# Scatters behind the casts, a third row buffer, the weights' parts moved, and drains between pages

## Chip, core and metric

The kernel runs on one core of one Trainium2 chip. The metric is the device time of one execution in microseconds (us), lower being better. TensorE is PE in the rows, VectorE DVE, ScalarE ACT, GpSimd POOL, SyncE SP; each works through its own instructions in order. DMAs are issued by SP (queue q1), by ACT for two first loads, and by GpSimd (queue q0).

## What is computed

Blockwise causal attention (8 batches, 8 heads, 576 positions, head size 64), whose output is the input of a mixture of 8 experts: each of 4608 rows goes to the one expert with the largest gate logit.

```python
scores = np.where(mask, scale * np.matmul(q, k.transpose(0, 1, 3, 2)), -1e9)  # mask: blocks of 64
attn_out = softmax(scores) @ v
x = attn_out.transpose(0, 2, 1, 3).reshape(B * S, H * D)        # 4608 x 512
logits = x @ w_gate
expert_idx, gate_w = argmax(logits), softmax(logits) at expert_idx
h = np.maximum(x_sorted[lo:hi] @ w1[e], 0.0)                     # rows of expert e: 512 -> 1024
y_sorted[lo:hi] = h @ w2[e]                                      # 1024 -> 512
out = gate_w[:, None] * y                                        # in the rows' first order
```

## The kernel before

Two stages overlap at their ends. The **attention stage** goes through 32 pairs of heads, four to a batch (`HP` = 4). Iteration `p` of the main loop does, in this order: loads ahead (`load_v` for pair p+4, `load` of q and k for pair p+6, all on SP; v's last 64 positions come for a whole batch in `load_v4`), GpSimd's `cast` of pair p+2 into the one buffer `h16`, the scatters and the loads of weights, `scores` of pair p+1, `attend`, `keep` and `sums` of pair p, TensorE's transposes of `h16` (`trans`, pair p+2), then `turn_back` and `finish` of pair p-1, which write the pair's 128 columns into the row buffer `x16s` of its batch, and at last `logits`, `denominators` and `settle` (a transpose by VectorE of the strip `sB`, line 323).

A batch is routed while the next is computed: `weigh` in step 0, `choose` in step 1, `ranks`, `gates` and `slots` in step 2 (iteration 4b+7 for batch b). After `slots` the batch's 576 rows, of 258 words each, go to the region of their expert in `xsorted`, by five indirect DMAs of GpSimd (`scatter`, lines 404 to 413): parts 0 and 1 at the end of step 2, parts 2 to 4 in step 3, ahead of the weights but behind that iteration's cast, and the parts 0 and 1 stand ahead of it. There are two row buffers, so batch b+2 writes what batch b's scatters read.

The weights are cast to half precision by GpSimd's DMAs, in 32 parts of 512 KB as written (`load_weights`, four to an expert): 24 parts in the attention stage, the other 8 in the first pages. `wall` holds them all, and the places of the last two experts are lent to attention until their parts come. `xsorted`'s first rows are cleared by one DMA (`clear_heads`).

Near the end of attention the first 20 pages (`FIRST`) are planned from the counts of batches 0 to 5: `first_counts` (VectorE), `first_turns` (five operations of GpSimd), `first_behind` (a comparison of VectorE, then a product of GpSimd), `first_rows` (VectorE). The first eight page loads (`mload`: a transposing DMA and a small one) are issued by SP in iteration 31; the very first waits for all scatters issued by then (`behind_all`), and the others stand behind it in SP's queue.

The **page stage** runs 36 to 63 pages of 128 rows. `page(T)` does the first product of page T (`m1`, 32 matmuls), stages the weights of page T+2 (`mstage`), does the second product of page T-1 (`m2`, 8 matmuls), whose result ScalarE writes to one of five `y` and GpSimd scatters to the output, and loads page T+6. The rows of batches 6 and 7 are routed beside the first pages.

Of the kernel before, what the change touches and what calls it, by code (L numbers as in the profile page):

```python
# [8 lines left out]
F32 = mybir.dt.float32  # L9
# [8 lines left out]
ROW = 258  # L18
# [4 lines left out]
def kernel(  # L23
# [30 lines left out]
    def sb(name, shape, dtype=F32):  # L54
        return pool.tile(shape, dtype, name=name)
# [20 lines left out]
    h16 = sb("h16", [128, 9, 128], F16)  # L76
    qkTs = [sb(f"qkT{i}", [128, 2, 576], F16) for i in range(2)]
    pts = [sb(f"pt{i}", [128, 2, 1408]) for i in range(2)]
    accs = [sb("acc", [128, 2, 640]),
            wall[:, E - 1, 8:16, :].rearrange("p a f -> p (a f)").bitcast(F32)[  # L80
                :, 0:1280].rearrange("p (h q) -> p h q", h=2)]
    p4s = [sb(f"p4_{i}", [128, 2, 64]) for i in range(2)]
    vts = [sb(f"v{i}", [128, 4, 2, 64]) for i in range(3)] + [
        guest[:, 2304 + i * 512:2816 + i * 512].rearrange("p (c h d) -> p c h d", c=4, h=2)
        for i in range(2)]
# [1 line left out]
    v4s = [sb("v4", [128, H, 64]), guest[:, 3328:3840].rearrange("p (h d) -> p h d", h=H)]  # L87
    oTs = [sb(f"oT{i}", [128, 640]) for i in range(2)]
    lr = sb("lr", [128, 160])
    x16s = [sb(f"x16_{i}", [128, 5, ROW], I32) for i in range(2)]  # L90
    lgp = sb("lgp", [128, 5, H, E])
    ohs = [sb(f"oh{i}", [128, 5, E], F16) for i in range(2)]
    recs = [sb(f"rec{i}", [128, 5, 2]) for i in range(2)]
# [59 lines left out]
    def tmp(name, w=E, dtype=F32):  # L153
        if name not in small:
            small[name] = sb(name, [128, w] if isinstance(w, int) else list(w), dtype)
        return small[name]
# [35 lines left out]
    def load_v4(b):  # L192
        nc.sync.dma_start(out=v4s[b % 2][64:128],
                          in_=v[b, :, 512:576, :].rearrange("h p d -> p h d"))
# [144 lines left out]

    def finish(p):  # L340
        b, hp = p // HP, p % HP
        x16 = x16s[b % 2].bitcast(F16)
        nc.vector.tensor_tensor(  # L343
            out=x16[:, :, hp * 128:hp * 128 + 128].rearrange("p i (h d) -> p i h d", h=2),
            in0=back[:, 0:640].rearrange("p (i h d) -> p i h d", h=2, d=64),
            in1=recs[p % 2].unsqueeze(3).to_broadcast([128, 5, 2, 64]), op=ALU.mult)
# [29 lines left out]
        nc.scalar.activation(tmp("ex", (128, 5, E)), tmp("d", (128, 5, E)), AF.Exp)  # L376

    def gates(b):
        x16, ex, sm = x16s[b % 2], tmp("ex", (128, 5, E)), tmp("sm", 5)
        nc.vector.reduce_sum(out=sm, in_=ex, axis=AX.X)  # L380
        nc.vector.reciprocal(x16.bitcast(F32)[:, :, 256], sm)
        nc.vector.tensor_single_scalar(x16[:, :, 257], ids, float(b * S), op=ALU.add)
# [20 lines left out]

    def scatter(b, j):
        m = 128 if j < 4 else 64
        slot = tmp(f"slot{j}_{b % 2}", 1, I32)
        nc.gpsimd.tensor_single_scalar(slot, small[f"sl{b % 2}"][:, j:j + 1], 128.0, op=ALU.add)  # L407
        did = nc.gpsimd.indirect_dma_start(  # L408
            out=xsorted[:, :],
            out_offset=bass.IndirectOffsetOnAxis(ap=slot[0:m, :], axis=0),  # L410
            in_=x16s[b % 2][0:m, j, :], in_offset=None)
        apart("rows", did)
        tc.declare_no_dep(did.ins, group="closed pages", reason="rows of pages not yet closed")

# [227 lines left out]
    with tc.manual_schedule(engines={ET.PE, ET.Activation, ET.DVE, ET.Pool, ET.SP}):  # L642
# [3 lines left out]
        load_v(0)  # L646
        load(2)
        load_v(1)
        nc.scalar.activation(warm, ident32[0:64, 64:65], AF.Exp)
        for _ in range(28):  # L650
            nc.tensor.transpose(sA16[:, 0:128], ident16, ident16)
# [8 lines left out]
        for h in range(2):  # L660
# [1 line left out]
            nc.sync.dma_start(  # L662
                out=gate[r], in_=moe_w_gate.rearrange("(p h d) e -> h d p e", h=2, d=64)[h])
            nc.gpsimd.tensor_copy(wg[r, :, h * E:h * E + E], gate[r, :, ::-1])
        slots_of = [p for p in range(2, PAIRS) if p % 4 or p < 8][:4 * PRESENT + 4]
        weights = {}
        for n, p in enumerate(slots_of):
            weights.setdefault(p, []).append(n)
        for p in range(PAIRS + 1):
            now, nxt, old = p < PAIRS, p + 1 < PAIRS, p > 0  # L670
            done, step = (p - 5) // HP, (p - 5) % HP if p > 4 else None
            left = PAIRS - p
            if p == 0:
                load_v4(0)
                for ahead in range(3, NQ + 1):
                    load(ahead)
                    load_v(ahead - 1)
            elif p + NV - 1 < PAIRS:
                load_v(p + NV - 1)
            if p + NQ + 1 < PAIRS:  # L680
                load(p + NQ + 1)
            if p % HP == 1 and p // HP + 1 < B:
                load_v4(p // HP + 1)
            if p + 2 < PAIRS:
                cast(p + 2)
            if step == 3:
                for j in range(2, 5):
                    scatter(done, j)
            for n in weights.get(p, ()):
                load_weights(n)  # L690
            if p == 1:
                routing_constants()
                clear_heads()
            if left == 1:
                for T in range(XS):
                    mload(T)
                mexpert(0, ET.Activation)
                mstage(0, nc.scalar)
            if nxt:
                scores(p + 1)  # L700
            if step == 2:
                shares()
            if now:
                if left == 2:
                    first_rows()
                attend(p)
                keep(p)
                sums(p)
            if step == 0:
                weigh()  # L710
            if step == 1:
                choose(done)
            if p == PAIRS:
                m1(0)
            turned = trans(p + 2) if p + 2 < PAIRS else None
            if step == 2:
                ranks(done)
            if old:
                turn_back(p - 1)
            if turned:  # L720
                turned()
            if step == 2:
                gates(done)
                slots(done)
                for j in range(2):
                    scatter(done, j)
            if left == 5:
                first_counts()
            if left == 4:
                first_turns()  # L730
            if left == 3:
                first_behind()
            if old:
                finish(p - 1)
                logits(p - 1, not now)
            if now:
                denominators(p, not old)
            settle(p)
            if left == 1:
                mexpert(1)  # L740
                mstage(1)
        rest = rest_pages()
        for T in range(N // 128):
            page(T, T > 0)
            if T < 4 * E - len(slots_of):
                load_weights(len(slots_of) + T)
            if T == 1:
                weigh()
                choose(B - 1)
                shares()  # L750
                gates(B - 1)
            if T == 3:
                ranks(B - 1)
                slots(B - 1)
            if 4 <= T < 9:
                scatter(B - 1, T - 4)
            if 4 <= T < 7:
                next(rest)
            if T == 12:
                pages = nc.values_load(total[0:1, 0:1], min_val=N // 128, max_val=PAGES,  # L760
                                       skip_runtime_bounds_check_because=why)
# [31 lines left out]
```

## Time and profile before

| | |
|---|---|
| median of 3 runs | 388.05 us (383.09 to 389.85) |
| the profiled execution | 384.53 us |
| its span, first to last instruction | 382.7 us |
| granted TensorE clock, mean | 0.965 |
| PE, DVE, ACT, POOL busy | 336.6, 238.0, 239.7, 178.9 us |
| read from HBM, written to it | 61.93 MB, 15.77 MB |

A busy time says how long an engine worked on its instructions, not that it was needed all that time. A wait ("its engine sat idle before it until") names the instruction, and behind the arrow what ended the idle time; three numbers are the total in us, how often, and the longest. In a timeline the idle time stands in brackets. PEclk is the granted share of full speed.

### The profile page before, as it was taken

The page shows a single profiled execution, that of the slowest core. Times are in us where ns is not written, and L with a number is a line of the kernel's source. Part 1 is how long each engine was busy: PE and PEld are TensorE (multiplying, and loading weights), DVE is VectorE, ACT ScalarE, POOL GpSimd, SP SyncE. Part 2 cuts the span into 40 slices and gives each one's busy share as a digit, 9 for nine tenths or more (in the row PEclk, how much of TensorE's full clock was granted, in tenths as well). Part 3 has the DMA queues.
Part 4 walks back from the last instruction along what each step waited for, and adds up shares of the span by engine and source line. Part 5 has one row for each costly group of instructions (what it writes and reads, how often), then busy time and mean ns, then how long its engine had stood idle before and what let it go on. Part 6 is the DMA issues. An engine that isn't in the chain of part 4 may idle for free. (4 is left out here: it accounts for less than half of the span.)

```text
span 382.7 us, 11499 instructions
## 1 busy us (share of the span) xinstructions
PE 336.6 (88%) x4232; PEld 227.5 (59%) x4232; DVE 238.0 (62%) x507; ACT 239.7 (63%) x533; POOL 178.9 (47%) x223
## 2 busy tenths in 40 slices
PE   5889997898789898898598798999999999999970
PEld 4556664556445556565355456777757777777740
DVE  3676888787668787888668688676324443343320
ACT  3888987787749687787567673545444544454440
POOL 3553135715713826718515815886845233223330
PEclk9999999999989999999879989999999999999995
DMA  8999999999999899999943196799998543443430
GB/s 189 224 222 250 231 233 236 264 237 239 267 188 200 195 216 229 203 226 205 202 78 70 40 182 93 130 194 236 229 194 197 141 114 93 112 126 92 102 112 13
DMA packets 96785, 67.02 MB, mean 175 GB/s; under 512 B 71760, under 2 KB 80976, under 8 KB 96720
## 3 DMA queue, kind: packets, MB, share of 16 engines
q1 hardware_dynamic: 78800, 34.62, 45.8%
q0 software_dynamic: 17632, 30.98, 39.5%
q8 instruction: 36, 0.59, 0.7%
q10 hardware_dynamic: 288, 0.59, 0.6%
q14 instruction: 29, 0.24, 0.2%
HBM read 61.93 MB, written 15.77 MB: 203 GB/s over the span
## 5 line engine op out<-in xcount | busy, mean ns | idle before, releaser
L587 DVE COPY pt<-wall 128x4096 f16 x39 | 48.2, 1236 | 61.2 <-PE sB L595 30.0
L595 PEld LDWEIGHTS <-pt 128*128 128x128 f16 x1216 | 70.9, 98 | 11.3 <-DVE pt L587 1.9
L408 POOL DMA_INDIRECT xsorted<-x,slot x40 | 49.2, 1231 | 12.8 <-POOL slot L407 10.5
L286 PE MATMUL oP<-pt,v 128*64 128x448 f32 (+2 forms) x320 | 52.8, 474 | 0.0
L615 POOL DMA_INDIRECT out_dram<-v,to x24 | 26.9, 1122 | 45.0 <-ACT v L611 41.4
L343 DVE TENSOR_TENSOR x<-sC,rec 128x640 f16<-128x640 f32 x32 | 26.3, 821 | 32.2 <-PE sC L337 22.4
L605 PEld LDWEIGHTS <-qkT 128*128 128x128 f16 x304 | 28.2, 98 | 27.1
L214 ACT ACTIVATE qkT<-sA 128x576 f16<-128x576 f16 x60 | 35.8, 648 | 13.5 <-PE sA L226 12.5
L216 POOL CAST h<-qk 128x1152 f16<-128x1152 f32 (+2 forms) x20 | 22.4, 1122 | 39.3 <-issue 27.8
L595 PE MATMUL sB<-qk,pt 128*128 128x128 f16 x608 | 37.0, 219 | 2.4 <-DMA qk<-xsorted 1.4
L286 PEld LDWEIGHTS oP<-pt,v 128*64 128x64 f32 x320 | 23.2, 142 | 25.1 <-issue 20.3
L407 POOL TENSOR_SCALAR slot<-sl 128x1 int32<-128x1 f32 x40 | 17.1, 428 | 42.7 <-DVE sl L402 36.8
L595 PE MATMUL sA<-qk,pt 128*128 128x128 f16 x608 | 37.1, 219 | 0.0
L246 ACT ACTIVATE pt<-sC 128x512 f32<-128x512 f32 (+2 forms) x96 | 32.6, 411 | 5.8 <-PE sC L241 5.8
L605 PE MATMUL sC<-wall,qkT 128*128 x152 | 35.9, 379 | 0.0
L605 PE MATMUL oP<-wall,qkT 128*128 x152 | 35.9, 379 | 0.0
L246 ACT ACTIVATE pt<-sB 128x768 f32<-128x768 f32 x64 | 34.8, 608 | 0.0
L600 ACT ACTIVATE qkT<-sB 128x1024 f16<-128x1024 f32 x19 | 19.5, 1024 | 24.4 <-PE sB L595 24.4
L600 ACT ACTIVATE qkT<-sA 128x1024 f16<-128x1024 f32 x19 | 19.4, 1024 | 22.8 <-PE sA L595 22.8
L286 PE MATMUL oP<-pt,wall 128*64 128x448 f32 (+2 forms) x192 | 31.4, 470 | 0.0
L226 PE MATMUL sA<-ident,h 128*128 128x128 f16 x270 | 20.3, 220 | 11.3 <-POOL h L216 11.3
L246 ACT ACTIVATE pt<-sA 128x896 f32<-128x896 f32 x32 | 29.4, 917 | 0.6 <-PE sC L241 0.2
(173 smaller groups left out, 597.4 us busy)
## 6 DMA issues: line engine op xcount, KB each, us to landing
wall<-in_moe_w_dram POOLq DMA_DIRECT2D x32, 512.0 KB, 9.1
qk<-in_q_dram SPq DMA_DIRECT2D x20, 288.0 KB
v<-in_v_dram SPq DMA_DIRECT2D x44, 128.0 KB
qk<-in_k_dram SPq DMA_DIRECT2D x18, 288.0 KB
wall<-in_v_dram SPq DMA_DIRECT2D x28, 128.0 KB
wall<-in_q_dram SPq DMA_DIRECT2D x12, 288.0 KB
wall<-in_k_dram SPq DMA_DIRECT2D x12, 288.0 KB
xsorted<-x SPq DMA_DIRECT2D x1, 1032.0 KB
```

Of the source, the lines that this page charges most:

```text
L214: nc.scalar.activation(dst, src, AF.Copy)
L216: engine.tensor_copy(dst, src)
L226: nc.tensor.transpose(ps[:, (c - c0) * 128:(c - c0) * 128 + 128], h16[:, c], ident16)
L246: nc.scalar.activation(dst, src, AF.Exp, scale=scale)
L286: nc.tensor.matmul(out=o[h * 64:h * 64 + 64], lhsT=vt[:, c, h, :] if c < 4 else v4[:, 2 * (p % HP) + h, :], rhs=src[:, h], start=(c == 0), ...
L343: nc.vector.tensor_tensor(out=x16[:, :, hp * 128:hp * 128 + 128].rearrange("p i (h d) -> p i h d", h=2), in0=back[:, 0:640].rearrange("p ( ...
L408: did = nc.gpsimd.indirect_dma_start(out=xsorted[:, :], out_offset=bass.IndirectOffsetOnAxis(ap=slot[0:m, :], axis=0), in_=x16s[b % 2][0:m ...
L587: else engine.tensor_copy(stages[T % 2], src)
L595: nc.tensor.matmul(out=hp[:, f // 4, f % 4 * 128:f % 4 * 128 + 128], lhsT=stages[T % 2][:, c * 1024 + f * 128:c * 1024 + f * 128 + 128], r ...
L600: nc.scalar.activation(hTs[T % 2], hp.rearrange("p a f -> p (a f)"), AF.Relu)
L605: did = nc.tensor.matmul(out=yp, lhsT=hT[:, f * 128:f * 128 + 128], rhs=wall[:, ds(pg["e", T], 1), 8 + f, :].rearrange("p a f -> p (a f)") ...
L615: did = nc.gpsimd.indirect_dma_start(out=out[:, :], out_offset=bass.IndirectOffsetOnAxis(ap=to, axis=0), in_=y, in_offset=None, bounds_che ...
```

## The change

- A third row buffer, in the lent place of the last expert's first weights; the two `p4` move into the place of its second weights. Batch b uses buffer b modulo 3.
- The scatters stand behind the cast of their iteration: from iteration 8 on, parts 0 and 1, then 2 and 3, then 4, in three iterations. Batch 6's come in iteration 32 and pages 0 and 1.
- Of the weights, 16 parts come in two of each three iterations from 3 to 25, and two each in iterations 27 to 30. The count before the pages stays 24.
- `load_v4` of the next batch is issued in a batch's first iteration and ahead of the other loads (before: in its second, behind them); the first one stands ahead of the main loop.
- `first_turns` (before in iteration 28) and `first_behind` (before behind iteration 29's `slots` place) both move to iteration 29, behind the cast and ahead of the scatters.
- GpSimd gets a drain after pages 12, 24 and 34.

```diff
-    accs = [sb("acc", [128, 2, 640]),
-            wall[:, E - 1, 8:16, :].rearrange("p a f -> p (a f)").bitcast(F32)[
-                :, 0:1280].rearrange("p (h q) -> p h q", h=2)]
-    p4s = [sb(f"p4_{i}", [128, 2, 64]) for i in range(2)]
+    last = wall[:, E - 1, 8:16, :].rearrange("p a f -> p (a f)").bitcast(F32)
+    accs = [sb("acc", [128, 2, 640]), last[:, 0:1280].rearrange("p (h q) -> p h q", h=2)]
+    p4s = [last[:, 1280 + i * 128:1408 + i * 128].rearrange("p (h q) -> p h q", h=2)
+           for i in range(2)]
...
-    x16s = [sb(f"x16_{i}", [128, 5, ROW], I32) for i in range(2)]
+    x16s = [sb(f"x16_{i}", [128, 5, ROW], I32) for i in range(2)] + [
+        wall[:, E - 1, 0:8, :].rearrange("p a f -> p (a f)").bitcast(I32)[
+            :, 0:5 * ROW].rearrange("p (j w) -> p j w", w=ROW)]
...
-        x16 = x16s[b % 2].bitcast(F16)
+        x16 = x16s[b % 3].bitcast(F16)
...
-        slot = tmp(f"slot{j}_{b % 2}", 1, I32)
+        slot = tmp(f"slot{j}_{b % 3}", 1, I32)
...
         load_v(1)
+        load_v4(0)
...
-        slots_of = [p for p in range(2, PAIRS) if p % 4 or p < 8][:4 * PRESENT + 4]
+        slots_of = [p for p in range(3, PAIRS - 5) if p % 3 < 2]
+        slots_of += [p for p in range(PAIRS - 5, PAIRS - 1) for _ in range(2)]
...
+        scatters = {}
+        for p in range(8, PAIRS + 1):
+            scatters[p] = ((0, 1), (2, 3), (4,), ())[p % HP]
...
+            if p % HP == 0 and p // HP + 1 < B:
+                load_v4(p // HP + 1)
             if p == 0:
-                load_v4(0)
...
-            if p % HP == 1 and p // HP + 1 < B:
-                load_v4(p // HP + 1)
             if p + 2 < PAIRS:
                 cast(p + 2)
-            if step == 3:
-                for j in range(2, 5):
-                    scatter(done, j)
+            if left == 3:
+                first_turns()
+                first_behind()
+            for j in scatters.get(p, ()):
+                scatter((p - 8) // HP, j)
             for n in weights.get(p, ()):
                 load_weights(n)
...
                 slots(done)
-                for j in range(2):
-                    scatter(done, j)
             if left == 5:
                 first_counts()
-            if left == 4:
-                first_turns()
-            if left == 3:
-                first_behind()
...
                 load_weights(len(slots_of) + T)
+            for j in ((2, 3), (4,))[T] if T < 2 else ():
+                scatter(B - 2, j)
...
+            if T in (12, 24, 34):
+                nc.gpsimd.drain()
```

## Rows read from the trace of the kernel before

**Rows 1.** The page, part 1: busy us (share of the span) and instructions.
```profile
PE 336.6 (88%) x4232; PEld 227.5 (59%) x4232; DVE 238.0 (62%) x507; ACT 239.7 (63%) x533; POOL 178.9 (47%) x223
```

**Rows 2.** Timeline of VectorE: start, us, operation; three of the 33 transposes of `settle`.
```profile
25.93 0.35 DVE L323 STREAM_TRANSPOSE lr<-sB 128x160 f32<-128x160 f32 x1
...
31.84 0.35 DVE L323 STREAM_TRANSPOSE lr<-sB 128x160 f32<-128x160 f32 x1 [0.16 <-PE oP L255]
...
233.07 0.34 DVE L323 STREAM_TRANSPOSE lr<-sB 128x160 f32<-128x160 f32 x1
```

**Rows 3.** Waits of PE from 26 to 233 us: total us, times, longest.
```profile
PE sA L226 <- POOL h L216: 11.3, 10, 2.7
PE sC L241 <- DVE x L343: 8.6, 5, 3.3
PE oP L286 <- DMA v<-in_v_dram: 2.4, 1, 2.4
```

**Rows 4.** Timeline of GpSimd from 86 to 101 us, one batch's scatters and two casts.
```profile
88.82 0.22 POOL L407 TENSOR_SCALAR slot<-sl 128x1 int32<-128x1 f32 x1 [5.05 <-DVE sl L402]
...
93.03 1.16 POOL L216 CAST h<-wall 128x1152 f16<-128x1152 f32 x1
94.16 0.27 POOL L407 TENSOR_SCALAR slot<-sl 128x1 int32<-128x1 f32 x1
...
99.96 1.16 POOL L216 CAST h<-qk 128x1152 f16<-128x1152 f32 x1
```

**Rows 5.** Timeline of PE and VectorE: the late `v4`, then a late row buffer.
```profile
67.35 0.34 PE L286 MATMUL oP<-p,v 128*64 128x64 f32 x4 [2.37 <-DMA v<-in_v_dram]
...
106.16 0.82 DVE L343 TENSOR_TENSOR x<-sC,rec 128x640 f16<-128x640 f32 x1 [3.89 <-DMA xsorted<-x,slot]
...
107.04 0.40 PE L241 MATMUL sC<-qkT 64*128 64x256 f16 x2 [3.33 <-DVE x L343]
```

**Rows 6.** Windows: length, busy us of the engines, PEclk, DMA share, GB/s.
```profile
60.00:103.00 43.00, 37.10 (x522) 23.65 (x524) 35.36 (x68) 32.94 (x87) 26.49 (x31) 1.00 1.14 253
103.00:116.00 13.00, 9.67 (x122) 5.62 (x116) 7.36 (x18) 7.16 (x20) 2.71 (x4) 0.87 0.95 201
116.00:184.00 68.00, 61.85 (x856) 39.60 (x852) 56.94 (x119) 55.42 (x151) 39.83 (x46) 1.00 1.05 210
184.00:202.00 18.00, 14.34 (x162) 8.48 (x164) 10.68 (x24) 10.29 (x28) 5.01 (x6) 0.81 0.79 135
...
216.00:233.00 17.00, 13.88 (x174) 8.92 (x175) 12.43 (x38) 9.91 (x19) 5.04 (x9) 0.90 0.91 125
```

**Rows 7.** A wait of SP's queue, and GpSimd's operations before pair 31's cast.
```profile
SPq L188 <- PE oP L286: 66.8, 16, 11.8
...
215.33 0.24 POOL L466 TENSOR_TENSOR left<-there,turn 128x20 f32<-128x20 f32 x1
...
217.07 1.15 POOL L216 CAST h<-qk 128x1152 f16<-128x1152 f32 x1
```

**Rows 8.** Pair 31's transposes to the first page: PE, one part, q0's traffic, SP.
```profile
218.27 0.68 PE L226 MATMUL sA<-ident,h 128*128 128x128 f16 x9 [2.71 <-POOL h L216]
...
L200 POOL DMA_DIRECT2D wall<-in_moe_w_dram x1: 853/853/853, 218.2 to 218.2; - x1
...
DMA to landing us min/median/max: 5.2/5.2/5.2
...
q0 software_dynamic: 1161, 1.23, 94.2%
...
223.41 1.34 SPq L568 DMA_TRANSPOSE qk<-xsorted  x1
...
232.79 1.96 PE L595 MATMUL sA<-qk,pt 128*128 128x128 f16 x32
```

**Rows 9.** GpSimd's drains (ns min/median/max) at the program's end, and its longest wait.
```profile
L788 POOLq DRAIN  x3: 51/103/4223, 377.7 to 382.5; - x3
...
POOL out_dram L615 <- ACT v L611: 41.4, 17, 4.9
```

More of the change, by code (lines that the diff above doesn't have):

```diff
@@ L378, in gates @@
     def gates(b):
-        x16, ex, sm = x16s[b % 2], tmp("ex", (128, 5, E)), tmp("sm", 5)
+        x16, ex, sm = x16s[b % 3], tmp("ex", (128, 5, E)), tmp("sm", 5)
         nc.vector.reduce_sum(out=sm, in_=ex, axis=AX.X)
@@ L410, in scatter @@
             out_offset=bass.IndirectOffsetOnAxis(ap=slot[0:m, :], axis=0),
-            in_=x16s[b % 2][0:m, j, :], in_offset=None)
+            in_=x16s[b % 3][0:m, j, :], in_offset=None)
         apart("rows", did)
```

## The prediction

> **What bounds the kernel now.** Read the page's first lines first: the kernel is a TensorE program, PE being busy 336.6 us, 88% of the span [rows 1]. But that is a mean over two stages. Part 4 of the page, the chain that ended last, holds almost only products of the page stage (the experts), one behind the other: nothing of this change makes a page cheaper. The attention stage before it must be read by itself, and the best ruler is `settle`'s transpose on VectorE, which comes once per pair of heads. The second of its 33 rows starts at 25.93 us, the third at 31.84, the 32nd at 233.07 [rows 2]. So an undisturbed pair takes 5.9 us, while 30 pairs took 207.1; 30 times 5.9 is 177.0. The attention stage thus loses 30 us, and the question is to what.
>
> The waits of PE between 26 and 233 us answer it [rows 3]: 11.3 us in ten waits for GpSimd's cast of `h16`, 8.6 us in five waits for VectorE's `x`, 2.4 us in one for `v`. That is 22.3. Most of the rest is the clock. The granted share is 1.00 in the quiet stretches, but 0.87 over the 13 us from 103, 0.81 over the 18 us from 184 and 0.90 over the 17 us from 216 [rows 6]: 1.7 + 3.4 + 1.7 = 6.8 us of full speed lost, in part at the lower level of 1.2 GHz, after PE had waited. Sum 29.1, nearly the 30.
>
> **Where each wait comes from.** GpSimd works in order. The timeline shows scatters 0 and 1 from 88.82 to 93.03, then a cast of 1.16, then scatters 2 to 4 from 94.16, and only at 99.96 the next cast [rows 4]. PE needs each cast 5.9 us after the last, so both casts of these two pairs are late, batch after batch: ten waits. The wait for `x` is a buffer's: `finish` of a batch's first pair writes the row buffer of two batches ago, and waits 3.89 us for its scatter's DMA; PE's scores wait 3.33 behind it [rows 5]. The clock drops of 103 and 184 lie right behind the two long waits of this kind. The wait for `v` is one on `load_v4`: it is the last product of `attend` that waits, the one with `p4` [rows 5].
>
> **The change, part by part.** All sums are made against the profiled execution: 384.5 us, span 382.7 and 1.8 around it. It lies 0.9% under the median of the three runs (388.05).
>
> *Casts first.* Every cast now stands ahead of the scatters of its pair, and a batch's five scatters are spread 2, 2, 1 over three pairs. In the worst pair GpSimd has a cast of 1.16, two scatters of 1.93 (5.80 us for three [rows 4]) and one part of weights, 0.85 [rows 8]: 5.9 us, just a pair. A cast may start some 4 us late before PE feels it (5.9 less 1.16 and the 0.7 us of transposes), so this fits. One piece remains: at pair 29 the cast of 31 now stands ahead of `first_turns`, five operations that took from 215.33 to 217.07 [rows 7], but VectorE's comparison in `first_behind` has moved ahead of that pair's `sums`, and waits for them with `sums`, `finish` and PE behind it. I put 0.7 us. Returned: 11.3 - 0.7 = 10.6.
>
> *Three row buffers.* The next writer of a buffer comes 13 pairs after the batch's start, its last scatter at pair 10 (counted alike): three pairs, 17.7 us, against a scatter that was late by 3.89. The two long waits go; the short ones, behind `first_counts` for one, stay. Of 8.6 I take 7.2 (bounds 6.3 and 8.6). `p4s` and the third buffer lie in the last expert's weights, whose parts are loaded only in pages 4 to 7: no cost, hidden by 30 us.
>
> *`load_v4` a pair earlier and ahead of the pair's other loads:* 2.4.
>
> *The clock.* The stretches at 103 and 184 go with the waits that they follow: 1.7 + 3.4 = 5.1. The third, at the end of the stage, I leave. Sum for attention: 10.6 + 7.2 + 2.4 + 5.1 = 25.3 us (bounds 20 and 29).
>
> *Weights.* The count before the pages stays 24, but now 16 until pair 25 and two each in pairs 27 to 30. So 0.7 instead of 0.75 parts per pair beside the loads, and a pile at the end. In front of the first page it costs. Count from the start of the transposes of pair 31 (218.27 before [rows 8]). GpSimd in pair 28: 1.16 + 3.9 + 1.7 = 6.7, so 0.8 late; cast, `first_turns`, `first_behind` and two scatters follow, and part 20 is issued at about +3.2. It lands 5.2 later [rows 8], at 8.4; part 21, on the same queue, 3.0 after it. (In the 8 us from 222 that queue moved 1.23 MB [rows 8], so 512 KB take 3.4 us; at the 253 GB/s of the best stretch [rows 6] 2.1; I take 3.0, near the row of the same stretch.) The batch's last scatter is issued behind them and lands at about 11.9. The first page's load waits for that scatter, as `behind_all` wants, and SP holds all page loads behind it. If it lands as a part does, 5.2 later, the first page is there at 17.1. PE stood at the first product 14.5 us after the transposes [rows 8]; 13.3 at full clock. Loss 3.8 us (bounds 0, with parts of 2.1 and a quick load; and 8.4, with parts of 3.4 and the 9.4 us from 223.41 to 232.79).
>
> That the scatter lands behind the parts is my reading of one queue. The Trainium skill says so too: DMA: Bandwidth & Descriptors, section Queues, rings and completion order, has each engine consume a ring's descriptors in ring order. By that rule the 3.8 us stand; were the scatter to pass the parts, there would be no loss and the sum would be 355.1.
>
> *Drains.* GpSimd's last drain took 4223 ns, after all page scatters; the two right behind it 103 and 51 [rows 9]. So it pays for something that has gathered, and drains at pages 12, 24 and 34 should pay it earlier. There they are hidden: in the page stage GpSimd waits 41.4 us for ScalarE's `y` alone [rows 9], and a late scatter only holds one of five `y`. I take 4.1 saved (bounds 0 and 4.2).
>
> One page speaks against this: the Trainium skill, VectorE: DVE Perf Modes, section The DRAIN you can't avoid, gives the drains around a program as about 12 ns, constant, on all engines. By it nothing gathers, nothing is saved, and the sum would be 363.0. The trace does not agree: 4223 ns beside 51.
>
> Sum: 384.5 - 25.3 + 3.8 - 4.1 = 358.9, say 359 us.
>
> **Rivals.**
> *The loads take over.* A pair now needs 885 KB of q, k and v, 350 KB of weights and 149 KB of scattered rows, 1.38 MB; in 5.9 us that is 235 GB/s. The best long stretch showed 253, the one from 116 us only 210 [rows 6]. Were 220 the limit, pairs would take 6.3 us; over some 20 pairs that is 8 us more: 367. Against it: over the stage SP's loads of v waited 66.8 us, in 16 waits, for `attend` to free a buffer [rows 7]: the loads waited for PE, not PE for them.
>
> *Slower than before: the loads had set the pace all along.* If 210 GB/s is all there is, pairs take 6.6 us, 30 of them 198 instead of 207: 9 us gained. Then the last loads share the queues with the eight parts; four more parts than before stand ahead of the scatter that the first page waits for, 13.6 us at 3.4 each, and the last drain stays: 384.5 - 9 + 13.6 = 389. It decides if the rate in pairs 9 to 25 stays under 215 GB/s. The 253 and the 66.8 speak against it.
>
> *The gate in front of the pages at its upper bound:* 8.4 instead of 3.8, 363.5.
>
> *The drains do not do what they are for:* the last one is a fixed cost: 363.
>
> **How the numbers follow.** The forecast as summed 0.60; loads in part 0.13; gate 0.10; drains 0.11; loads all along, or worse, 0.06. A measurement of this kernel tells about 2% from no change. Only the last case is not faster by that: faster 0.94, same 0.04, slower 0.02. Low end: all attention waits and clock returned, no gate: 384.5 - 29.1 - 4.1 = 351.3; with the other terms rarely all at this bound, 352. High end: 367, the loads in part. That leaves out about 0.15.
>
> **What would show it.** Right: `settle`'s transposes 5.9 us apart through pairs 8 to 26, the 32nd near 207; no wait of PE for `h` above 1 us and no `x` waiting for a scatter; PEclk 1.00 from 26 to 190 us; a wait of some 4 us of the first page's product for `xsorted`; a last drain under 0.5 us. Wrong: pairs of 6.3 us or more with waits for q, k or v; a first product more than 8 us late; a last drain of 4 us; waits of the page scatters at pages 12, 24 and 34 that reach PE.

## The result, and the profile after

The changed kernel took 364.4 us (median of four runs, 361.2 to 369.1) where the kernel before took 386.9 (median of four, 383.1 to 389.9): a ratio of 0.942, 95% interval 0.930 to 0.955. The forecast was 359 us, 352 to 367. The profiled execution took 361.18 us, with a span of 359.4. Measured again later, in a second set, the changed kernel took 368.7 us beside 382.6, a ratio of 0.966 (0.958 to 0.974). Some executions of either kernel are slower, so medians of the second set, like all ratios, are of those within 1.5% of the kernel's fastest (there five of six and five of eleven, in that set's other kernels three and two of six). So the gain is between 3 and 7%, and not as sharp as one set of runs makes it look; where the time between the two sets lies is told under the last experiment.

Part 1 of the page after, to set beside [rows 1]:

```profile
PE 332.7 (93%) x4232; PEld 227.7 (63%) x4232; DVE 225.5 (63%) x507; ACT 239.5 (67%) x533; POOL 178.4 (50%) x223
```

The same 4232 matmuls, 3.9 us less of busy time, and a span 23 us shorter: the work has hardly become less, the gaps have. To see where, take the ruler of [rows 2], VectorE's transpose in `settle`, in the timeline of after (its line is L325 now):

```profile
26.05 0.35 DVE L325 STREAM_TRANSPOSE lr<-sB 128x160 f32<-128x160 f32 x1
31.95 0.35 DVE L325 STREAM_TRANSPOSE lr<-sB 128x160 f32<-128x160 f32 x1 [0.16 <-PE oP L257]
...
176.86 0.35 DVE L325 STREAM_TRANSPOSE lr<-sB 128x160 f32<-128x160 f32 x1 [0.16 <-PE oP L257]
184.58 0.33 DVE L325 STREAM_TRANSPOSE lr<-sB 128x160 f32<-128x160 f32 x1
...
208.00 0.34 DVE L325 STREAM_TRANSPOSE lr<-sB 128x160 f32<-128x160 f32 x1
218.36 0.34 DVE L325 STREAM_TRANSPOSE lr<-sB 128x160 f32<-128x160 f32 x1
```

The 30 pairs between the second row and the 32nd took 208.00 - 26.05 = 181.95 us, against 207.14 before: 25.2 saved. But the 33rd row follows 10.36 us behind the 32nd; before, 3.3 us lay between them. Something new stands there.

The waits of PE from 26 to 208 us, as in [rows 3] (waiting line, what ended the wait, total us, times, longest):

```profile
PE sC L243 <- DVE x L345: 2.6, 4, 1.6
PE sC L243 <- DVE wall L345: 0.7, 2, 0.4
PE mix L389 <- ACT oT L295: 0.6, 1, 0.6
```

The 11.3 us for the cast `h` and the 2.4 for `v` are gone; of 8.6 for `x` some 3.3 are left (one of three buffers is called `wall` now, since it lies there). In the windows (stretch, then busy us and instructions of each engine, PEclk, DMA share, GB/s) the clock stays full to 200 us:

```profile
60.00:103.00 43.00, 42.07 (x585) 27.16 (x583) 35.27 (x81) 37.53 (x100) 27.26 (x32) 1.00 1.15 252
...
180.00:200.00 20.00, 18.45 (x263) 12.02 (x259) 16.84 (x46) 16.60 (x46) 16.11 (x22) 1.00 0.73 124
200.00:212.00 12.00, 6.64 (x90) 4.37 (x89) 9.41 (x28) 4.88 (x5) 6.40 (x8) 0.93 1.18 193
212.00:230.00 18.00, 15.94 (x181) 12.71 (x181) 8.97 (x23) 6.17 (x8) 9.11 (x11) 0.86 0.99 150
```

**The new gap.** The timeline around the first page; the first row is the transposes of pair 31, from which the forecast counted, then GpSimd's parts 20 and 21 of the weights and batch 5's last scatter behind them, SP's first page load, and PE:

```profile
194.05 0.68 PE L228 MATMUL sA<-ident,h 128*128 128x128 f16 x9
...
197.22 1.58 POOL L202 DMA_DIRECT2D wall<-in_moe_w_dram  x2
...
199.71 1.38 POOL L410 DMA_INDIRECT xsorted<-wall,slot  x1 [0.29 <-POOL slot L409]
...
206.91 1.31 SPq L570 DMA_TRANSPOSE qk<-xsorted  x1
...
206.53 0.73 PE L312 MATMUL sB<-wall,picks 128*32 128x160 f32 x16
213.29 3.57 PE L597 MATMUL sA<-qk,pt 128*128 128x128 f16 x32 [6.04 <-DMA qk<-xsorted]
```

The weights leave GpSimd 3.2 us behind the transposes, the load of the first page 12.9, PE is ready at 13.2 and starts at 19.2, after a wait of 6.04. Then the product takes 3.57 us, where later ones take 1.95: the granted clock had fallen, 0.86 over 212 to 230 us, and 0.50, its lower level of 1.2 GHz, over the product itself (213.2 to 216.9 us).

**The end.** The last product of PE, before and after (timelines):

```profile
368.42 1.89 PE L605 MATMUL sC<-wall,qkT 128*128 x8
```

```profile
349.94 1.89 PE L607 MATMUL sC<-wall,qkT 128*128 x8
```

From the first page's product to the end of this one are 137.5 us before ([rows 8] has the 232.79) and 138.5 after. From there to the span's end it is 12.4 and 7.6. GpSimd's drains explain most of the last (executions: shortest, median and longest ns; then the first and last start):

```profile
L764 POOLq DRAIN  x3: 3698/5140/5854, 266.9 to 340.3; - x3
...
L794 POOLq DRAIN  x3: 55/103/436, 358.1 to 359.1; - x3
```

The last long one took 436 ns where it took 4223 [rows 9].

| part of the span | forecast | measured |
|---|---|---|
| up to the second `settle` | 0 | +0.1 |
| 30 pairs | -25.3 | -25.2 |
| from the 32nd `settle` to the first page's product | +3.8 | +5.6 |
| page stage | 0 | +1.0 |
| behind the last product | -4.1 | -4.8 |
| sum | -25.6 | -23.3 |

The fourth number is 213.29 - 208.00 = 5.29 against 232.79 - 233.07 = -0.28.

### The profile page after: what moved, and what is told of

It reads as the page before. It is cut to its first block, busy times and chain, and to the rows that moved or that the text cites. A ratio compares the mean times of both kernels' runs of the same rounds, so it can differ in the third digit from the quotient of the medians.

```text
span 359.4 us, 11498 instructions
## 1 busy us (share of the span) xinstructions
PE 332.7 (93%) x4232; PEld 227.7 (63%) x4232; DVE 225.5 (63%) x507; ACT 239.5 (67%) x533; POOL 178.4 (50%) x223
## 4 chain that ended last, share of the span: by engine, by line
PE 73%; DMA 10%; POOL 5%; DVE 4%; issue 4%; SPq 1%; ACT 0%; DVEq 0%; POOLq 0%; ACTq 0%
PE oP L288 18%; PE sA L597 9%; PE sC L607 8%; PE sB L597 8%; PE oP L607 8%; DMA qk<-xsorted 7%; PE sB L312 6%; PE sA L228 4%; PE sC L339 3%; PE mix L288 3%; PE sB L243 2%; DMA qk<-in_q_dram 2%; PE sC L243 2%; DMA wall<-in_k_dram 1%; POOL xsorted L410 1%
## 5 line engine op out<-in xcount | busy, mean ns | idle before, releaser
L597 PEld LDWEIGHTS <-pt 128*128 128x128 f16 x1216 | 72.5, 99 | 16.5 <-issue 8.4
L288 PE MATMUL oP<-pt,v 128*64 128x448 f32 (+2 forms) x320 | 50.8, 459 | 0.0
L597 PE MATMUL sA<-qk,pt 128*128 128x128 f16 x608 | 38.7, 224 | 6.9 <-DMA qk<-xsorted 6.9
L410 POOL DMA_INDIRECT xsorted<-x,slot x30 | 36.4, 1214 | 9.3 <-POOL slot L409 7.9
L345 DVE TENSOR_TENSOR x<-sC,rec 128x640 f16<-128x640 f32 x24 | 19.7, 822 | 20.7 <-PE sC L339 19.1
L288 PE MATMUL oP<-pt,wall 128*64 128x448 f32 (+2 forms) x192 | 30.4, 459 | 0.0
L617 POOL DMA_INDIRECT out_dram<-oT,to x14 | 15.0, 1069 | 26.1 <-ACT oT L613 16.4
L218 POOL CAST h<-wall 128x1152 f16<-128x1152 f32 x12 | 13.8, 1151 | 26.2 <-PE sA L228 20.1
```

Source lines behind the costliest of these rows:

```text
L218: engine.tensor_copy(dst, src)
L288: nc.tensor.matmul(out=o[h * 64:h * 64 + 64], lhsT=vt[:, c, h, :] if c < 4 else v4[:, 2 * (p % HP) + h, :], rhs=src[:, h], start=(c == 0), ...
L345: nc.vector.tensor_tensor(out=x16[:, :, hp * 128:hp * 128 + 128].rearrange("p i (h d) -> p i h d", h=2), in0=back[:, 0:640].rearrange("p ( ...
L410: did = nc.gpsimd.indirect_dma_start(out=xsorted[:, :], out_offset=bass.IndirectOffsetOnAxis(ap=slot[0:m, :], axis=0), in_=x16s[b % 3][0:m ...
L597: nc.tensor.matmul(out=hp[:, f // 4, f % 4 * 128:f % 4 * 128 + 128], lhsT=stages[T % 2][:, c * 1024 + f * 128:c * 1024 + f * 128 + 128], r ...
L617: did = nc.gpsimd.indirect_dma_start(out=out[:, :], out_offset=bass.IndirectOffsetOnAxis(ap=to, axis=0), in_=y, in_offset=None, bounds_che ...
```

## Experiments: which part brings the attention stage's gain

Theory: the third buffer and the casts, each worth about what its waits and the clock behind them cost. Rivals: the loads, the early `load_v4` or the weights' new schedule carry part of it.

**The third buffer alone.** The kernel before with only this of the change (the two `p4` move as well):

```diff
+        wall[:, E - 1, 0:8, :].rearrange("p a f -> p (a f)").bitcast(I32)[
+            :, 0:5 * ROW].rearrange("p (j w) -> p j w", w=ROW)]
...
-        x16 = x16s[b % 2].bitcast(F16)
+        x16 = x16s[b % 3].bitcast(F16)
```

> The kernel before with the third row buffer alone (and p4 moved with it); scatters, weights and v4 as before, no drains. Theory: the two long waits for x (3.3 and 3.0 us of PE) and the slow clock behind them go, 11 to 12 us in all, ratio about 0.97; the ten waits for casts (11.3 us) stay. Rival, the late scatters only shift the wait elsewhere, to the casts: gain under 4 us.

Measured 377.6 us beside 384.0, ratio 0.986 (0.979 to 0.993). The 30 pairs took 194.25 us, 12.9 less than in the profile of before; the forecast has 7.2 for this buffer and 5.1 for the clock behind its waits, 12.3. Waits of PE from 26 to 212 us:

```profile
PE sA L228 <- POOL h L218: 12.7, 12, 2.7
...
PE sC L243 <- DVE x L345: 1.0, 1, 1.0
PE oP L288 <- DMA v<-in_v_dram: 0.4, 1, 0.4
```

No scatter holds `x` any more, and the waits for the casts stay, as expected. The span, 374.8 us, fell less than the stage, by 7.9: this execution reached its second `settle` 2.1 us later than that of before, and took 1.4 more in the page stage and 1.3 more behind it. Of the 12.9, 2.0 us are the wait for `v`, which this edit does not touch, while the waits for casts grew by 1.4. And the long waits for `x` do not come at the same pairs in each execution, as the next experiment suggests. So 12.9 is the difference between two single profiles; by the times the part is worth 1.4% (0.7 to 2.1), some 5.5 us.

**The early `load_v4` alone**, on the kernel before:

```diff
+        load_v4(0)
...
+            if p % HP == 0 and p // HP + 1 < B:
+                load_v4(p // HP + 1)
...
-            if p % HP == 1 and p // HP + 1 < B:
-                load_v4(p // HP + 1)
```

> The kernel before with load_v4 an iteration earlier and ahead of the other loads, nothing else. Theory: pair 8 loses its 2.4 us wait for v4, the other pairs keep theirs, so the 32nd transpose of settle comes some 2.5 us earlier. Rival, the wait is a sign that the loads are behind as a whole and moves to q, k or v: the 32nd transpose stays where it was.

One execution: 384.6 us beside a median of 384.0. PE's waits, 26 to 230 us:

```profile
PE sA L226 <- POOL h L216: 13.3, 12, 2.7
PE sC L241 <- DVE x L343: 7.4, 5, 5.0
```

The wait for `v` is gone, and the pair where it stood takes 7.07 us in place of 8.49. No time follows from that: in this execution the next pair waited 5.0 us for `x`, at a place where the profile of before has a wait of 0.9. A single execution cannot price an edit of 2 us.

**Buffer and casts together**, with the weights, `first_turns` and `load_v4` as before and no drains (the scatters stay in their new table). Against the changed kernel, in its main lines:

```diff
-        slots_of = [p for p in range(3, PAIRS - 5) if p % 3 < 2]
-        slots_of += [p for p in range(PAIRS - 5, PAIRS - 1) for _ in range(2)]
+        slots_of = [p for p in range(2, PAIRS) if p % 4 or p < 8][:4 * PRESENT + 4]
...
-            if T in (12, 24, 34):
-                nc.gpsimd.drain()
```

> The kernel before with the third row buffer and the scatters behind the casts over three iterations; weights, v4 and first_turns as before, no drains. Theory: beside the 11 to 12 us of the buffer the waits for casts go, another 10 to 11 us; what is left of the pairs is the v4 wait of 2.4 us at pair 8: ratio about 0.945. The wait before the pages is as small as with the old weights. Rival, without the earlier v4 and the fewer parts the loads fall behind: PE waits for q, k or v by more than 5 us.

Measured 366.7 us, ratio 0.955 (0.948 to 0.961). The 30 pairs took 183.1: 11.1 less than with the buffer alone (10.6 were forecast for the casts), and 1.2 more than with the whole change. Of this, 0.8 is the wait for `v`, 2.4 before. So buffer and casts carry the gain of the stage, and by the medians (366.7 and 364.4, of two sets of runs) all the rest of the change nets to some 2 us, less than the 3.8 that its drains take off the end.

## Experiments: the weights' schedule

Theory: two parts in each of pairs 27 to 30 put a pile of transfers in front of the first page, which costs the 6.04 us, and the lighter load ahead of it (0.7 parts per pair in place of 0.75) buys nothing. Rival: it buys undisturbed loads.

**The old schedule in the changed kernel**, run in two sets on two chips (the `slots_of` edit just shown, and nothing else):

> The changed kernel with the weights' parts as before (three of four iterations from 2, one each near the end); everything else as changed. Theory that the pile of eight parts makes the 6.0 us wait in front of the pages, and that 16 instead of 19 parts until iteration 25 matter little as the loads are not the bound: the wait goes, pairs stay at 5.9 us, the time falls by some 5 us. Rival, the loads are near the bound: with the old parts PE waits for q, k or v in pairs 8 to 26 by 5 us or more, and the two about cancel.

> The changed kernel with the weights' schedule of before, again, since the intervals of the two overlapped. Theory A, the new schedule costs at the first page's gate and buys nothing: 2 to 4 us faster than the changed kernel beside it, first-page waits of 3 to 5 us in place of 6. Theory B, the difference was chance: within 1 us of it.

First: 361.4 us, ratio 0.934 (0.923 to 0.945). Second: 366.6, ratio 0.956 (0.945 to 0.966), beside 368.7 for the changed kernel. The 30 pairs took 181.5 and 182.8 us (0.9 of the latter in its first pair), 182.0 in the changed kernel: they hardly differ. What differs is the first page; PE's first product with the old schedule, first and second set, and in the changed kernel of the second set (of the last two some matmuls have no record, so their lengths are not to be compared):

```profile
210.08 3.46 PE L597 MATMUL sA<-qk,pt 128*128 128x128 f16 x32 [3.14 <-DMA qk<-xsorted]
```

```profile
214.02 2.26 PE L597 MATMUL sA<-qk,pt 128*128 128x128 f16 x26 [3.60 <-DMA qk<-xsorted]
```

```profile
213.67 2.61 PE L597 MATMUL sA<-qk,pt 128*128 128x128 f16 x23 [5.89 <-DMA qk<-xsorted]
```

Counted from the 32nd `settle`, the product starts 2.3 and 2.8 us behind it with the old schedule, 5.3 and 5.2 with the new one. So the new schedule loses 2.4 to 3 us at the gate. Not all of that is lost in the time: with the old schedule the page stage behind it took 0.7 and 1.2 us longer in these executions, so that the last product starts some 2.2 and 1.1 us earlier, counted from the 32nd `settle`. The ratios go the same way (0.934 against 0.942, 0.956 against 0.966), but their intervals overlap, so by the times alone it is not settled.

**The pile behind the scatters.** If the pile were only ahead of batch 5's last scatter in the queue, it should be enough to issue it behind:

```diff
-        slots_of += [p for p in range(PAIRS - 5, PAIRS - 1) for _ in range(2)]
+        slots_of += [PAIRS - n for n in (5, 4, 2, 1) for _ in range(2)]
```

> The changed kernel with the last four parts of weights moved from iterations 29 and 30 to 30 and 31, behind the last scatter of batch 5. Theory that parts 20 and 21 stand ahead of that scatter in one queue and so hold the first page: the last scatter lands some 3 us after its issue instead of 6, the first page load is issued about 5 us earlier, PE's wait of 6.0 us for it falls under 1 us, and the time falls by 5 us. Rival, the first page waits for the planning (first_rows) or for SP: the wait stays near 6 us and so does the time.

Measured 365.2 us, ratio 0.944 (0.938 to 0.951): no change. The timeline, page loads and the first product:

```profile
202.68 1.62 SPq L570 DMA_TRANSPOSE qk<-xsorted  x1
205.91 1.25 SPq L570 DMA_TRANSPOSE qk<-xsorted  x1
208.28 3.17 SPq L570 DMA_TRANSPOSE qk<-xsorted  x1
212.78 3.96 SPq L570 DMA_TRANSPOSE qk<-xsorted  x1
...
213.81 3.57 PE L597 MATMUL sA<-qk,pt 128*128 128x128 f16 x32 [4.10 <-DMA qk<-xsorted]
```

and its window from 212 us:

```profile
212.00:230.00 18.00, 12.82 (x121) 10.75 (x121) 7.48 (x18) 3.43 (x5) 6.67 (x9) 0.72 1.33 133
```

The 32nd `settle` of this execution was at 210.43, so the first load is issued 7.8 us ahead of it, where the changed kernel has 1.1. That much was the order on the queue. The Trainium skill, DMA: Bandwidth & Descriptors, section Queues, rings and completion order, has a ring's descriptors consumed in ring order. It says so of the queues of SP and ACT, and adds that a later descriptor may finish its write before an earlier one, so that it does not by itself promise the landing behind the parts that the forecast took from it. The trace agrees with that landing on GpSimd's queue: with the scatter out of the parts' way, the load that waits for it is issued 6.7 us earlier. But the load now takes 11.1 us to PE's product (202.68 to 213.81), not 6.4 (206.91 to 213.29), and the fourth to the seventh load come 4.2 to 5.1 us behind the one before, not 2.3 to 2.4: the four parts were issued between 201.17 and 204.27 us, beside it. (This execution took 368.7 us, the longest of its five, so the usual load may lose less.) The same section says that each DMA engine takes packets in turn from the queues that have work; by it, a parts' pile costs a page load time wherever it stands close by, and these rows agree. The forecast knew the first of the two costs and not the second.

**The pile ahead of it all**, one part in nearly every pair from 2 on:

```diff
-        slots_of = [p for p in range(3, PAIRS - 5) if p % 3 < 2]
-        slots_of += [p for p in range(PAIRS - 5, PAIRS - 1) for _ in range(2)]
+        slots_of = [p for p in range(2, PAIRS - 4) if p not in (12, 20)]
```

> The changed kernel with all 24 parts in iterations 2 to 27, one each but for 12 and 20, so none in the last four. Per pair 885 KB of loads, 524 of a part and 149 of scatters, 264 GB/s at 5.9 us, above the best long stretch of before (253). Theory that parts in the way of the first page cost the wait there (6.0 us with eight at the end, 3.1 with three): the wait falls under 1.5 us, pairs stay at 5.9 as the prefetch bridges the shortage, time 5 to 8 us below the changed kernel. Rival, the loads are near the bound: PE waits for q, k or v in the pairs by 5 us or more, and nothing is won.

Measured 363.6 us, ratio 0.945 (0.939 to 0.950): no change against the changed kernel. The execution profiled took 367.7, the longest of four. In it the first page does not wait at all; the pairs pay for it, 186.4 us for 30, the six of 17 to 22 taking 6.0 to 7.5 us. GpSimd's timeline shows one load that was late:

```profile
140.46 1.14 POOL L218 CAST h<-qk 128x1152 f16<-128x1152 f32 x1 [9.95 <-DMA qk<-in_k_dram]
```

GpSimd had nothing to do for 9.95 us, until `k` was loaded. PE waited 1.5 us for that cast. The other waits that grew are those for `x`, 6.1 us against 3.3: the casts now ran at other times, and some of VectorE's operations do not get on beside a cast (line 331's product took 0.60 us on the mean between 118 and 165 us, 0.18 in the changed kernel; see the part on what is left). So the rival of the forecast in which the loads take over shows in one wait: not at 0.7 parts per pair (235 GB/s by the forecast's count), where no pair waits for a load, but at about one, 500 KB for each pair instead of 350, some 260 GB/s counted alike. And the page stage gives back some more (window 230 to 260):

```profile
230.00:260.00 30.00, 25.69 (x278) 19.24 (x276) 15.32 (x43) 11.29 (x15) 21.10 (x23) 0.90 1.30 183
```

PE works 25.7 of 30 us there, 30.0 in the changed kernel. None of the four schedules is free: the bytes are paid in the pairs, at the gate or in the first pages.

## Experiments: the drains

Theory: GpSimd's last drain pays for what was gathered since the one before. Rival: the changed kernel's short drain has another cause, or the earlier drains cost the pages what the last one saves.

**No drains:**

```diff
-            if T in (12, 24, 34):
-                nc.gpsimd.drain()
```

> The changed kernel without its three drains. Theory that a drain pays for the DMAs issued since the last one (436 ns after 5, 4223 ns after 110): the last drain takes 4.2 us again and the time rises by 3.8 us, ratio to the kernel before about 0.952 instead of 0.942. Rival, the time before the last drain is what changed and the drain itself is fixed: no change. Second rival, the drains of 3.7 to 5.9 us between the pages hold the page scatters: the pages get faster without them, by up to 1 us.

**One behind page 12:**

```diff
-            if T in (12, 24, 34):
+            if T == 12:
```

> The changed kernel with only the drain after page 12, so 27 DMAs of GpSimd lie between it and the last drain. Theory by count (0.26 us and 36 ns for each DMA, from 436 ns after 5 and 4223 ns after 110): the last drain takes 1.2 us. Rival, a price paid once, at the first drain after DMAs: 0.44 us or less.

**One behind page 24:** the same edit with 24.

> The changed kernel with the drain behind page 24 alone. After none in the pages the last drain took 4223 ns, after one behind page 12 it took 2247, after the one behind page 34 it took 436. Theory A, it grows with the page scatters since the last drain, some 82 ns for each between the last two: 1.1 to 1.4 us here. Theory B, the count of all of GpSimd's DMAs of the whole program sets it in proportion (4223 over about 110): 0.5 to 0.8 us. Theory C, any drain in the pages but a far one pays it all: 0.44 us.

Measured 368.1 us (ratio 0.952, 0.945 to 0.959); 366.3 and 368.4, one execution each. The last drains, in that order (shortest, median, longest of the three at the end):

```profile
L792 POOLq DRAIN  x3: 51/103/4223, 360.8 to 365.5; - x3
```

```profile
L794 POOLq DRAIN  x3: 51/103/2247, 361.4 to 364.2; - x3
```

```profile
L794 POOLq DRAIN  x3: 51/103/1257, 364.5 to 366.3; - x3
```

The traces show 4 page scatters behind the last of the three drains (the changed kernel, 436 ns), 14 behind the one of page 24 (1257) and 26 behind the one of page 12 (2247), one fewer than the expectations count: (1257 - 436) / 10 = 82 ns and (2247 - 1257) / 12 = 83 ns for each. The third point was forecast from the other two, at 1.1 to 1.4 us. A line through them is shown; where it ends is not: with no drain there are 38 page scatters, for which it gives 2247 + 12 x 83 = 3.2 us, and 4223 was measured, the same in kernels with different schedules of weights and scatters (4222 with the third buffer alone). So what ahead of the page scatters counts, and how, stays open.

The drains in the pages cost nothing that can be seen: they take 3.7 to 5.9 us each in the changed kernel, but behind them GpSimd only has scatters to issue, and PE waits for none of them. Without drains the page stage, from the first product to the last, took 137.3 us, with them 138.5; the same stage took 137.5 to 141.9 in two executions where nothing of it was changed (the kernel before, and with the early `load_v4`), so no cost can be told. The 3.8 us less of drain at the end are about the difference of the medians, 368.1 - 364.4, which are of two sets of runs, and the intervals of the two ratios overlap: the time agrees, and the drain itself is what the traces show.

## Experiments: what is left of the attention stage's loss

The 30 pairs take 182 us, the undisturbed ones 5.90 (177.0 for 30). Nearly all of the 5 us lies in six pairs: 6.45 to 6.53 us in 7, 11, 15, 19 and 23, where VectorE does `gates` and `slots` ahead of `finish`, and 7.72 in pair 27 (`first_counts`). Theory: late `finish` holds PE, so move the bookkeeping behind it. Rival: VectorE is late for the next pair then.

```diff
-            if step == 2:
-                gates(done)
-                slots(done)
-            if left == 5:
-                first_counts()
...
             settle(p)
+            if step == 2:
+                gates(done)
+                slots(done)
+            if left == 5:
+                first_counts()
```

(with the old weights' schedule)

> As the one before, and gates, slots and first_counts moved behind settle, the last work of VectorE in an iteration, so that finish is not late. Theory A, what is left of the attention stage's loss is this bookkeeping ahead of finish: pairs 7, 11, 15, 19 and 23 fall from 6.5 to 5.9 or 6.0 us and pair 27 from 7.7 to about 6, 30 pairs take 177 to 178 us, 4 to 5 us less than the one before. Theory B, VectorE is then late for the next pair's sums and denominators and the wait only moves: 181 to 182 us, no change of time.

> The changed kernel, measured once more beside the next two. The pairs have cost 5.90 us, but 6.5 where a batch's gates and slots stand ahead of finish on VectorE (pairs 7, 11, 15, 19, 23) and 7.7 where first_counts does (27). Both theories: 361 to 366 us, 30 pairs in about 182 us, a wait of the first page's product of about 6 us.

Measured 369.9 us, ratio 0.968 (0.955 to 0.982), beside 366.6 (0.956, 0.945 to 0.966) for the same kernel without the move. The intervals overlap, so a loss is not shown by the times; the gain of 4 to 5 us did not come. In the profiles the 30 pairs took 187.7 us against 182.8, 5 more. PE's waits from 26 to 212 us, and the steps at pairs 22, 23 and 24:

```profile
PE mix L257 <- DVE pos L403: 9.9, 6, 1.7
```

```profile
159.00 0.35 DVE L325 STREAM_TRANSPOSE lr<-sB 128x160 f32<-128x160 f32 x1 [0.16 <-PE oP L257]
165.08 0.35 DVE L325 STREAM_TRANSPOSE lr<-sB 128x160 f32<-128x160 f32 x1 [0.16 <-PE sB L312]
172.57 0.35 DVE L325 STREAM_TRANSPOSE lr<-sB 128x160 f32<-128x160 f32 x1
```

The wait for `x` is gone and pair 23 takes 6.08. Then pair 24 takes 7.49: `slots` reads the ranks from `mix`, and line 257, the next pair's scores, writes into `mix`. They are different columns of it, 192 to 239 read and 128 to 191 written, so no value is overwritten, and the wait is for the tile as a whole; the ranks in a tile of their own were not tried. Neither theory had this tile in it: the one forecast a gain, the other no change. Six such waits, 9.9 us, took the place of some 3 for `x`. The place of the bookkeeping is a compromise that this move does not beat.

Both theories also miss what the bookkeeping costs where it stands. The kernel before has it in the same place, and its pairs 7, 11, 15, 19 and 23 took 6.01 to 6.02 us. What is new is a cast of GpSimd beside it (changed kernel, GpSimd and then VectorE, and the same operation in the kernel before):

```profile
132.82 1.15 POOL L218 CAST h<-qk 128x1152 f16<-128x1152 f32 x1 [4.05 <-issue]
```

```profile
133.25 0.77 DVE L403 TENSOR_TENSOR pos<-pos,oh 128x40 f32<-128x40 f32 x1
134.12 0.20 DVE L404 TENSOR_REDUCE sl<-pos 128x5 f32<-128x40 f32 x1
134.23 0.81 DVE L345 TENSOR_TENSOR x<-sC,rec 128x640 f16<-128x640 f32 x1
```

```profile
L401 DVE TENSOR_TENSOR pos<-pos,oh x8: 189/192/193, 60.2 to 247.9; 128x40 f32<-128x40 f32 x8
```

An operation of 0.19 us takes 0.77 and ends within 0.1 us of the cast's end, in pairs 7, 11, 15, 19, 23 and 27 alike, and `finish` (line 345) stands behind it. Behind `settle`, in the kernel with the move, it takes 0.19 again. The first profile with the old weights' schedule has both cases: in pair 7 the cast starts at 60.67, behind the product's start at 60.55, the product takes 0.19 and the pair 6.01; in pair 11 the cast is ahead (83.83 and 84.26), the product takes 0.77 and the pair 6.46. So some 0.5 us in each of six pairs, about 3 us of the 5, come from the cast's new place. Moving the cast or that product apart was not tried.

The changed kernel took 368.7 us in this set. Its profiled execution (366.3 us, 5.1 above the one shown first) has the pairs of the first (181.97 us) and the same wait at the gate (5.89, quoted above); 0.5 us more are spent ahead of the pairs, 1.3 behind the last product, and 3.4 in the page stage: its last product starts 140.05 us behind the first one, 136.65 in the execution shown first. PE's waits behind the first product are 5.0 us there, 1.7 in the execution shown first, which is nearly all of the 3.4; the longest of them:

```profile
265.27 1.95 PE L597 MATMUL sB<-qk,pt 128*128 128x128 f16 x32 [2.02 <-DMA qk<-xsorted]
```

The three other kernels of this set had page stages of 143.2 to 144.0 us (141.9 here), the one without drains behind pages 12 and 34 too, so these are not its cause. Why the page stage took longer in this set, while the kernel before took less (382.6 against 386.9), was not found out.

## Why the forecast came out as it did

*Casts, buffer and clock: right in mechanism; in size the close agreement is in part luck.* The sum for the stage was 25.3 and came out at 25.2, against the one profile from which it was summed. The buffer alone gave 12.9 (forecast 12.3 with the clock), of which 2.0 were the wait for `v`; the casts on top of it 11.1 (10.6); the rest of the change 1.2, 0.8 of it the wait for `v` (2.4). Yet by the times the buffer is worth some 5.5 us, and the kernel before with an early `load_v4` took 202.3 us for its 30 pairs, 4.8 less than the profile counted from, where the forecast gives 2.4 to that edit: a stage that differs by 2 us and more between executions cannot confirm a tenth. The piece that was to be left of the casts' wait, 0.7, was not seen, and of the wait for `x` 3.3 us stayed where 1.4 were put. The forecast let the cast go ahead at no cost; that it would hold a product of VectorE ahead of `finish`, 0.5 us in each of six pairs, was not in it.

*Loads in part, and loads all along: no.* The stretch from 60 to 103 us moved 252 GB/s with PE busy 42.07 of 43 us. 210 GB/s, where the trace of before was slowest, was not a limit but what was asked for; at about one part per pair one load came late. (The forecast's 350 KB of weights for a pair are nearer 367, 0.7 of 524 KB, so 237 GB/s and not 235; nothing hangs on it.)

*The gate: right in place, undersized.* Up to the scatter each step came as worked out: parts at +3.2 (3.2), PE ready at +13.2 (13.3). Then the load was issued at +12.9, where the scatter had been put at 11.9, and took 6.4 us to the product, not 5.2: a wait of 6.0 in place of 3.8. And the slow first product is a cost the forecast had left out: PE came out of its wait at a lower clock, as it had in the trace of before behind both its long waits [rows 6]. The experiments have it alike: 3.46 us for this product behind a wait of 3.14, 1.96 without a wait (the pile ahead of it all).

*Weights: costed, but not weighed.* The forecast took the new schedule as given and put a price only on its pile. That the old schedule in the changed kernel would wait 3 us instead of 6 could have been worked out from the same rows.

*Drains: right.* 4.1 forecast, 3.8 from the drain itself and 1.0 elsewhere behind the last product. The page of the Trainium skill that the forecast weighed against this, VectorE: DVE Perf Modes, section The DRAIN you can't avoid (about 12 ns, constant, on all engines), speaks of drains that the runtime sets. The ones here the profile lists at lines of the program, and GpSimd's took 436 to 4223 ns at the end, 3.6 us and more amid the pages: the page's figure is not theirs.

What the sum came to lack, 2.3 us, is the gate with its slow product and the page stage. That compares two profiles; the median, 364.4, is 5.4 above the forecast, and 3.2 of that is that the profiled execution was the fastest of its four. The second set of runs lies outside the forecast's range; its profile puts two thirds of its distance from the first into the page stage, where the forecast had allowed for no difference between executions.

## What to carry to other kernels

When an engine that works in order issues both a short step that the bottleneck needs and long transfers, put the step first; and give a buffer that transfers read a full cycle more than they need: the two together brought most of what this stage had to give. A transfer moved out of the way in its queue still shares the DMA engines with what it was moved behind: cost its bytes, not only its place. When an operation moves on one engine, look at what another engine does at its new time. Before moving bookkeeping on an engine, list which tiles it reads and who writes them next.

## What the runs showed of the hardware

- GpSimd's last drain grew by 82 to 83 ns for each page scatter since the drain before (436, 1257, 2247 ns after 4, 14, 26), and was 4223 ns without one. A drain between the pages took 3.6 to 9.6 us, and by the gaps between GpSimd's page scatters the one behind page 12 was the longest in each run that had more than one (5.9, 7.3 and 9.6 us among them).
- With the third buffer alone, 30 pairs took 12.9 us less, of which some 5 us were not waits of PE but the clock that had fallen behind them. Behind the waits of 3.33 and 3.04 us of the kernel before it was 0.87 over 13 us and 0.81 over 18; in the changed kernel 1.00 was granted from 26 to 200 us, where PE's longest wait was 1.6 us.
- A product of VectorE that takes 0.19 us by itself took 0.77 when it began inside a cast of GpSimd (1.15 us), and ended with it, six times in one execution. Not every operation is held: line 401's took its usual 0.20 us in the same cast, at 132.93.
- With four 512 KB parts of the weights in flight beside it, a page's transposing load took 11.1 us to PE's product instead of 6.4.
